# A re-tuned instruction order, with the second W1 split by column halves and exp's bias of two batches on GpSimd

## The chip, the cores and the metric

The kernel runs on one core of a Trainium2 chip. The metric is the device time of one execution, in microseconds (us). A core has five engines with a queue of instructions each: TensorE (PE in the profile, its weight loads PEld), VectorE (DVE), ScalarE (ACT), GpSimd (POOL) and SyncE (SP), which issues all transfers here.

## The reference

Three blocks follow each other, on 4 batches of 576 rows and 512 columns.

```python
# 1. attention, 8 heads of 64, with only the 32 largest scores of a row kept
scores = q @ k.T / 8
kth    = the 32nd largest score of the row
attn   = softmax(where(scores >= kth, scores, -1e9))
x      = attn @ v                                   # heads side by side: (4, 576, 512)
# 2. Fourier mixing and an FFN
u  = x + real(fft(fft(x, axis=1), axis=2))
x  = u + relu(layernorm(u) @ w_ch1) @ w_ch2         # 512 -> 2048 -> 512
# 3. a second FFN with its own weights and a gain g_ln
x  = x + relu(layernorm(x) * g_ln @ w_ch1') @ w_ch2'
```

The weights arrive as 64-bit floats. Products of fp16 pairs (a high and a low half of each value) stand in for fp32 products.

## The kernel before, in words

The function `tile_attention_fourier_ffn` doesn't issue instructions at once. It records them in a `Program`, and a planner (`Program.order`, line 336 on) then places all of them in one fixed order for each engine. At every step it takes, of the instructions whose inputs and buffers are planned to be ready, the one that can start first; among those that could start together the one with the lowest priority number. The planned duration of each instruction comes from `price` (line 289 on), with a doubled price for TensorE when it has had too few columns lately (line 397). Priorities come from the table `LEVELS`: for each named phase five numbers, one for each engine in the order TensorE, VectorE, ScalarE, GpSimd, SP, and five slopes by which the number changes over the phase's instructions. `PACE` gives the earliest times of the loads and splits of weights (first time, step, first time of the split, step), and of the statistics of the inputs (s1 to s3).

The phases are: `p0` to `p3` prepare a head's q, k and v; `a0`, `b0` and so on are the two halves of a batch's attention; `e`, `f`, `c` are the Fourier rows and columns; `g`, `o` the layer norms; `m` the first FFN, `n` the second FFN; `w1a`, `w2a`, `w2b`, `w1b` load and convert the four weights (1a and 2a of the first FFN, 1b and 2b of the second), and `x1a` and so on split them into fp16 halves. In program order each batch's attention comes first, then its Fourier part and norms (`front`), then the two FFNs; the planner mixes the attention of batch b + 1 into the FFNs of batch b.

Attention (`attend`) handles 36 tiles of 128 query rows for a batch. TensorE makes the scores, ScalarE copies them to s, and VectorE finds the 32 largest by four MAX8 (mx) with three replacements between (a value load and a replacement, which write w). Then VectorE makes nb, the bias of exp, from the largest and the 32nd value: one column of 128 rows, shown as `tiny<-mx` (batch 0, whose scale is a constant) or `tiny<-mx,sc` (the others). ScalarE goes on with Prelu (`s<-s,mx`), exp (`s<-s,tiny`), which needs nb, and an fp16 copy p; GpSimd subtracts to get p's low half; SP transposes p to pt, and TensorE multiplies by v (`xp<-vt,pt`).

An FFN works on 256 rows (tiles A and B of a batch) or 128 (C, for the odd rows of two batches). For each of 16 blocks f of 128 hidden columns TensorE adds up 12 matmuls of W1 into a buffer of the tag mm (three buffers), ScalarE and GpSimd (VectorE in the last batch) make the halves of h (two buffers), and TensorE multiplies h by block f of W2. A block f reads W1's columns `fs` of half `f // 8`, for all four blocks `dc` of 128 rows. W1A, W2A and W1B stay in SBUF. W2 of the second FFN is kept in DRAM (W2D) and loaded block by block into tiles of the tag ws.

W1B's memory serves as staging space for the other weights until the fourth weight itself is loaded. That weight is then split in 8 chunks c of 1024 columns: chunk c holds rows block `c // 2` and column half `c % 2`. Each chunk has two parts of 512 columns. For a part ScalarE makes a scaled copy in a tile of the tag ws (`ws<-W1B,tiny`) and its fp16 high half (`W1B<-ws`), and GpSimd subtracts to get the low half (`W1B<-ws,W1B`). The tag ws has two buffers and, unlike the other tags, a single queue for all streams, so that its tiles are handed out in program order: first the raw words of the fourth weight, then the split's 16 parts, then the W2 blocks of the second FFN.

```python
        P.tag(name, nbytes, bufs, split=name != "ws")                       # line 474
        vt.queue = vt.tag.queues.setdefault(self.stream if vt.tag.split else "", [])   # line 284
            t = P.tile("ws", [128, 2, 512], F16)                            # line 1128, W2 of the second FFN
            sp.dma_start(out=t, in_=W2D[f])
```

Of the kernel before, what the change touches and what calls it, by code (L numbers as in the profile page):

```python
# [17 lines left out]
ALU = mybir.AluOpType  # L18
# [50 lines left out]
LEVELS = {'a0': (99, 178, 7, -140, 441, -52, 95, 45, -105, 270), 'a1': (-20, -99, 572, -2, -218, -142, 122, 184, -28, 77), 'a2': (-140, 579, -502, -147, 161, 21, 207, 85, 77, -182), 'a3': (-142, -62, 142, 637, 122, 18, 53, 50, 48, -50), 'const': (231, 276, -510, -32, 217, 199, -207, -198, 71, -11), 'e0': (137, -39, 42, -496, -277, 78, -57, 145, 59, -79), 'e1': (-51, 334, -544, -257, -279, 132, -197, 53, 220, 260), 'e2': (-501, 419, -430, -171, 209, -156, 116, -65, -91, -198), 'e3': (-524, 499, -134, -294, 380, -27, 66, 153, 40, -249), 'f0': (-110, 178, -342, 181, 82, -229, -83, -408, 166, 132), 'f1': (-399, 429, -93, -94, 191, 0, 245, 49, -108, 292), 'f2': (273, -472, -408, 45, 230, 89, 100, 70, 74, 36), 'f3': (-2, 28, 455, -446, -130, -137, 253, -14, 146, 26), 'm0': (75, -18, 248, -377, 396, 74, -225, -112, -24, -36), 'm1': (152, 359, -246, 528, -356, 200, -79, 158, 237, 13), 'm2': (352, -165, -189, -571, -113, -58, -32, -342, 15, -203), 'm3': (-432, -110, 548, -8, 58, 20, -195, -2, 200, -97), 'n0': (309, -620, -101, -184, 37, 84, 20, 312, -12, -64), 'n1': (472, -201, -160, 434, 18, 148, 194, -185, -49, -73), 'n2': (687, -146, -140, 636, 597, 136, 246, -63, -112, -156), 'n3': (670, 195, -133, 501, -300, 192, -83, 35, -158, -54), 'p0': (496, -621, 26, -170, -181, 7, 22, 17, -189, -75), 'p1': (420, 240, 189, 49, 382, -103, -5, -4, 83, -42), 'p2': (-142, 595, 495, 433, 824, -135, 21, 44, -4, -67), 'p3': (-166, 268, 411, -177, 301, -41, -35, 2, -90, -8), 'st0': (-133, -139, -87, -43, -414, -199, -98, -174, -106, 123), 'st1': (226, -333, 107, 35, -411, 99, -86, 312, -76, -15), 'st2': (-218, -203, 88, -366, 295, 123, -208, 4, 20, -60), 'st3': (-10, -68, 146, 208, 57, -189, -296, 99, -5, 22), 'sv0': (445, -86, -414, 331, -306, -171, 81, -18, -39, 91), 'w1a': (-96, -235, 543, 89, 145, -109, 22, 66, -21, 118), 'w1b': (-152, -500, 48, -6, -4, 207, 98, -16, 95, -180), 'w2a': (-334, -79, 25, 129, -16, 11, 130, 47, 14, -322), 'w2b': (-310, 7, 32, -650, -5, -3, 92, -167, -21, 51), 'b0': (-186, 280, -343, 51, 33, -85, 55, -52, 51, 89), 'c0': (-170, -344, -7, -124, -47, 34, 25, 94, -286, -3), 'g0': (364, -83, 534, -267, 171, 160, -53, 31, 173, 97), 'o0': (383, -151, -46, -64, -263, 3, -235, 43, 13, -54), 'b1': (-394, 461, 138, 131, -208, 27, 123, 86, -103, -70), 'c1': (-238, -803, -221, 201, -273, 139, 98, -130, 117, -69), 'g1': (-305, 194, 401, 9, -254, -52, -157, -163, -141, -36), 'o1': (161, 224, 48, -340, 317, -147, 78, 159, -50, -154), 'b2': (177, 545, 171, -131, 9, -139, 122, 156, 137, -47), 'c2': (366, -97, -56, 425, 398, 67, 69, -96, -23, 217), 'g2': (-280, -259, 470, -171, 212, -46, -46, 108, 109, 40), 'o2': (596, 339, -84, 199, 45, 216, 91, -25, -381, -27), 'b3': (-90, 64, -217, 248, 308, 181, 127, 237, 261, 31), 'c3': (689, 64, 316, 592, -294, 57, -175, -53, 117, 1), 'g3': (341, 155, 274, 9, -9, -202, 128, -162, -10, 50), 'o3': (-280, -313, 364, -250, -37, 4, -74, -140, 253, 11), 'x1a': (32, 105, 264, 122, -133, 14, -77, -180, 36, -173), 'x2a': (-423, -381, -359, -381, -276, 19, -71, 333, -45, 227), 'x1b': (-433, -288, 222, 112, 290, -24, -91, -71, -65, 3), 'x2b': (263, -69, 295, 26, -182, 126, -245, 41, 166, -94)}  # L69
PACE = {'1a': (7.0, 4.0, 60.0, 6.5), '2a': (8.0, 5.0, 88.0, 1.5), '2b': (31.0, 10.0, 0.0, 8.5), '1b': (87.0, 14.0, 119.0, 9.5), 's1': (83.0, 4.5, 230, 0.5), 's2': (127.0, 3.0, 670, 8.0), 's3': (3.0, 1.0, 100, 2.5)}  # L70


def rows_ap(t, first, step, n, width):
# [123 lines left out]
class Program:  # L197
# [138 lines left out]
    def order(self):  # L336
# [108 lines left out]
def tile_attention_fourier_ffn(ctx: ExitStack, tc: tile.TileContext, q, k, v, w1a, w2a, g, w1b, w2b, c1_in, c2_in, c2l_in, out):  # L445
# [182 lines left out]
    def load_weight(nm, W, src, raws, tmps, t0, step, t1, step1):  # L628
# [609 lines left out]
```

## Time and profile before

| | |
|---|---|
| time, median of 3 runs | 1324.04 us (1323.81 to 1325.63) |
| the profiled execution's own time | 1330.46 us |
| its span, first to last instruction | 1328.7 us |
| TensorE busy | 1182.6 us, 89% |
| VectorE busy | 993.0 us, 75% |
| ScalarE busy | 846.0 us, 64% |
| GpSimd busy | 680.2 us, 51% |
| mean granted TensorE clock | 0.94 of full speed |

The shares are averages over the whole span, and the stages have different limits, so the rows further down are taken by stretches of time. Busy time is the time in which at least one instruction of the engine is on record; durations of neighbouring records on an engine can overlap. A wait is put down to the instruction that released it. All instructions carry the line of the planner's emit loop, L433, so that tiles' names, not lines, tell the groups apart. Matmul records at the lower of the two clock levels are about twice as long.

### The profile page before, as it was taken

The page shows a single profiled execution, that of the slowest core. Times are in us where ns is not written, and L with a number is a line of the kernel's source. Part 1 is how long each engine was busy: PE and PEld are TensorE (multiplying, and loading weights), DVE is VectorE, ACT ScalarE, POOL GpSimd, SP SyncE. Part 2 cuts the span into 40 slices and gives each one's busy share as a digit, 9 for nine tenths or more (in the row PEclk, how much of TensorE's full clock was granted, in tenths as well). Part 3 has the DMA queues.
Part 4 walks back from the last instruction along what each step waited for, and adds up shares of the span by engine and source line. Part 5 has one row for each costly group of instructions (what it writes and reads, how often), then busy time and mean ns, then how long its engine had stood idle before and what let it go on. Part 6 is the DMA issues. An engine that isn't in the chain of part 4 may idle for free.

```text
span 1328.7 us, 27154 instructions
## 1 busy us (share of the span) xinstructions
PE 1182.6 (89%) x9422; PEld 748.8 (56%) x9422; DVE 993.0 (75%) x2361; ACT 846.0 (64%) x1888; POOL 680.2 (51%) x1015
## 2 busy tenths in 40 slices
PE   7757888676799749999999999979999999999998
PEld 3433444342566525656666766656666666667665
DVE  6999999939899998999967986999996651214112
ACT  4658888467878897787767786777777652122111
POOL 3666343646777776666756564766645452011000
PEclk9999788578799869999999999999999999999999
DMA  6898655978867656876826376699514735014112
GB/s 186 193 263 222 178 129 122 264 189 234 196 162 158 121 120 153 174 170 141 177 62 110 68 175 164 141 217 189 105 22 97 163 90 129 13 24 126 27 33 56
DMA packets 356085, 184.86 MB, mean 139 GB/s; under 512 B 293225, under 2 KB 321002, under 8 KB 355818
## 3 DMA queue, kind: packets, MB, share of 16 engines
q1 hardware_dynamic: 355946, 183.11, 59.0%
q8 instruction: 74, 1.21, 0.4%
q14 instruction: 65, 0.53, 0.1%
HBM read 101.78 MB, written 14.16 MB: 87 GB/s over the span
## 4 chain that ended last, share of the span: by engine, by line
PE 63%; DVE 11%; DMA 7%; ACT 6%; issue 2%; POOL 2%; SPq 2%; POOLq 0%; ACTq 0%; DVEq 0%
PE mm L433 31%; PE acc L433 24%; PE ps L433 4%; PE xp L433 4%; DVE mx L433 4%; DVE w L433 3%; DMA pt<-p 2%; DMA ws<-W2D 2%; ACT s L433 2%; SPq L433 2%; DMA W1B<-in_moe_w_ch_dram 2%; DVE tiny L433 1%; DVE W1B L433 1%; DVE W2A L433 1%; ACT W1B L433 1%
## 5 line engine op out<-in xcount | busy, mean ns | idle before, releaser
L433 DVE MAX8 mx<-w 128x8 f32<-128x576 f32 x432 | 314.3, 747 | 1.3
L433 POOL TENSOR_TENSOR p<-s,p 128x64 f16<-128x64 f32 (+1 forms) x288 | 208.1, 743 | 118.2 <-ACT p L433 106.5
L433 ACT ACTIVATE h<-mm 128x256 f16<-128x256 f32 (+1 forms) x320 | 115.7, 362 | 212.7 <-PE mm L433 181.0
L433 PEld LDWEIGHTS <-h 128*128 128x128 f16 x1728 | 161.7, 98 | 141.6 <-issue 7.0
L433 PE MATMUL mm<-unT,W1B 128*128 128x256 f16 (+1 forms) x1920 | 220.7, 263 | 6.0 <-ACT W1B L433 3.4
L433 PE MATMUL mm<-unT,W1A 128*128 128x256 f16 (+1 forms) x1920 | 221.3, 263 | 1.1 <-DMA unT<-t2k 0.6
L433 PE MATMUL acc<-W2A,h 128*128 128x512 f16 x864 | 216.9, 379 | 1.4 <-POOL h L433 1.2
L433 POOL TENSOR_TENSOR h<-hr,h 128x256 f16<-128x256 f32 (+1 forms) x224 | 143.9, 646 | 140.1 <-ACT h L433 78.9
L433 PEld LDWEIGHTS <-W1B 128*128 128x128 f16 (+1 forms) x1984 | 176.8, 99 | 67.3 <-POOL W1B L433 13.9
L433 DVE MATCH_REPLACE8 w<-mx,w 128x576 f32<-128x576 f32 x288 | 212.8, 740 | 0.0
L433 PEld LDWEIGHTS <-W1A 128*128 128x128 f16 (+1 forms) x1984 | 177.5, 99 | 60.1 <-POOL W1A L433 8.1
L433 PE MATMUL acc<-ws,h 128*128 128x512 f16 x654 | 165.9, 380 | 6.2 <-DMA ws<-W2D 5.6
L433 DVE SCALAR_TENSOR_TENSOR h<-mm,h 128x256 f16<-128x256 f32 (+1 forms) x96 | 36.4, 379 | 171.8 <-ACT h L433 142.9
L433 DVE MAX8 mx<-s 128x8 f32<-128x576 f32 x144 | 107.5, 747 | 53.9 <-ACT s L433 53.6
L433 ACT ACTIVATE s<-s,mx 128x576 f32<-128x576 f32 x144 | 111.0, 773 | 22.2 <-DVE mx L433 21.9
L433 ACT ACTIVATE hr<-mm 128x256 f32<-128x256 f32 (+1 forms) x224 | 82.1, 368 | 65.0 <-PE mm L433 53.8
L433 PE MATMUL xp<-vt,pt 128*128 128x65 f16 (+1 forms) x2240 | 106.0, 203 | 16.5 <-DMA pt<-p 13.7
L433 PEld LDWEIGHTS <-pt 128*128 128x128 f16 (+1 forms) x2240 | 94.6, 107 | 44.9 <-DMA pt<-p 22.9
L433 ACT ACTIVATE s<-ps 128x576 f32<-128x576 f32 x144 | 93.6, 650 | 39.9 <-POOL p L433 21.8
L433 DVE MATCH_REPLACE8 w<-mx,s 128x576 f32<-128x576 f32 x144 | 106.6, 740 | 0.0
L433 PE MATMUL ps<-kt,qt 128*128 128x512 f16 (+5 forms) x512 | 90.2, 320 | 18.3 <-ACT s L433 18.2
L433 ACT ACTIVATE p<-s 128x576 f16<-128x576 f32 x144 | 97.6, 683 | 2.4 <-DMA pt<-p 1.9
(155 smaller groups left out, 1643.2 us busy)
## 6 DMA issues: line engine op xcount, KB each, us to landing
ws<-W2D SPq DMA_DIRECT2D x118, 256.0 KB
W1B<-in_moe_w_ch_dram SPq DMA_DIRECT2D x56, 512.0 KB
n<-in_q_dram SPq DMA_DIRECT2D x32, 128.0 KB
n<-in_k_dram SPq DMA_DIRECT2D x32, 128.0 KB
n<-in_v_dram SPq DMA_DIRECT2D x32, 128.0 KB
W2F<-W1B SPq DMA_DIRECT2D x16, 256.0 KB
ws<-in_moe_w_ch_dram SPq DMA_DIRECT2D x16, 256.0 KB
W1B<-W2F SPq DMA_DIRECT2D x16, 256.0 KB
```

Of the source, the lines that this page charges most:

```text
L433: getattr(getattr(self.nc, op.eng), op.method)(*[fix(a) for a in op.args], **{k: fix(v) for k, v in op.kw.items()})
```

## The change

Four things change.

- The split of the fourth weight (W1B) takes its chunks in the order 0, 2, 4, 6, 1, 3, 5, 7: first the first column half of all four blocks of rows, then the second half. The order in which its tiles of ws are asked for follows.
- nb of batches 0 and 1 is made on GpSimd; batches 2 and 3 keep VectorE.
- Two prices of the planner change: a replacement's fixed part on VectorE from 168 to 112 ns, and TensorE's price after few columns from twice the price to twice the price plus 25 ns.
- All numbers of LEVELS and PACE are replaced, and the Fourier constants may be loaded from 168 us on instead of 183.

In the diff, LEVELS is one long line for each side; of it a few entries are shown, each on a line of its own.

```diff
-SMALL = "dve"
+SMALL = (0, 1)
...
-LEVELS = {
+LEVELS = {
...
-'f1': (-399, 429, -93, -94, 191, 0, 245, 49, -108, 292)
+'f1': (-86, 422, 309, 152, 178, 42, 293, 57, -21, 295)
...
-'p1': (420, 240, 189, 49, 382, -103, -5, -4, 83, -42)
+'p1': (412, -138, 185, 52, 416, -162, 102, -7, 76, -16)
...
-'b1': (-394, 461, 138, 131, -208, 27, 123, 86, -103, -70)
+'b1': (-451, 482, 130, 72, 48, 46, 249, 94, -93, -72)
...
-'x1b': (-433, -288, 222, 112, 290, -24, -91, -71, -65, 3)
+'x1b': (-628, -341, 195, -119, 200, -108, -221, -70, -101, -89)
...
-PACE = {'1a': (7.0, 4.0, 60.0, 6.5), '2a': (8.0, 5.0, 88.0, 1.5), '2b': (31.0, 10.0, 0.0, 8.5), '1b': (87.0, 14.0, 119.0, 9.5), 's1': (83.0, 4.5, 230, 0.5), 's2': (127.0, 3.0, 670, 8.0), 's3': (3.0, 1.0, 100, 2.5)}
+PACE = {'1a': (0.0, 4.5, 8.0, 2.0), '2a': (7.0, 3.5, 120.0, 0.0), '2b': (82.0, 1.5, 0.0, 13.0), '1b': (87.0, 16.0, 0.0, 59.0), 's1': (82.0, 0.5, 230, 0.5), 's2': (16.0, 12.0, 670, 8.0), 's3': (162.0, 10.5, 100, 2.5)}
...
-            op.cost = (168 if op.method == "match_replace" else 76 if op.method in ("tensor_scalar", "tensor_tensor") else 66) + 57 * fields + n / (1.92 if fast else 0.96)
+            op.cost = (112 if op.method == "match_replace" else 76 if op.method in ("tensor_scalar", "tensor_tensor") else 66) + 57 * fields + n / (1.92 if fast else 0.96)
...
                 if columns.get(k - 1, 0) < enough:
-                    op.cost *= 2
+                    op.cost = 2 * op.cost + 25
...
-    sm, rv = getattr(P, SMALL), getattr(P, FLIP)
+    rv = getattr(P, FLIP)
...
-        for c in range(8):
-            P.at(t1 + c * step1, (nm, 2, c))
+        for i, c in enumerate(range(8) if nm != "1b" else (0, 2, 4, 6, 1, 3, 5, 7)):
+            P.at(t1 + i * step1, (nm, 2, i))
...
-            parts = [tmps(2 * c + j) for j in range(2)]
+            parts = [tmps(2 * i + j) for j in range(2)]
...
         nb = tiny(1)
-        sm.tensor_scalar(out=nb, in0=mx[:, 31:32], scalar1=mx[:, 0:1], scalar2=scale(b, "c"), op0=ALU.subtract, op1=ALU.mult)
+        (gp if b in SMALL else dve).tensor_scalar(out=nb, in0=mx[:, 31:32], scalar1=mx[:, 0:1], scalar2=scale(b, "c"), op0=ALU.subtract, op1=ALU.mult)
...
-        P.at(183)
+        P.at(168)
```

## Rows read from the trace of the kernel before

**Rows 1.** Busy time in stretches: PE, PEld, DVE, ACT, POOL, then clock, DMA.

```profile
26.00:133.00 107.00, 75.95 (x402) 38.89 (x400) 104.11 (x235) 74.58 (x138) 67.17 (x67) 1.00 0.85 222
133.00:266.00 133.00, 106.43 (x636) 54.81 (x636) 122.40 (x282) 98.68 (x190) 60.05 (x75) 0.74 0.64 173
...
345.00:451.00 106.00, 104.27 (x943) 71.22 (x943) 101.75 (x256) 87.92 (x205) 76.43 (x118) 0.99 0.70 160
451.00:471.50 20.50, 11.44 (x102) 6.75 (x99) 20.47 (x48) 20.34 (x41) 19.48 (x30) 0.67 0.74 131
471.50:500.00 28.50, 10.91 (x98) 5.65 (x99) 27.86 (x61) 26.08 (x55) 20.46 (x28) 0.64 0.55 113
500.00:1064.00 564.00, 542.88 (x4907) 361.58 (x4907) 476.86 (x1123) 413.80 (x970) 347.37 (x564) 0.99 0.64 137
1064.00:1328.70 264.70, 259.46 (x1970) 174.93 (x1968) 70.49 (x187) 58.89 (x160) 36.13 (x45) 0.99 0.25 63
```

**Rows 2.** Tile ws: durations in ns (min/median/max), first and last start in us.

```profile
L433 PE MATMUL acc<-ws,h x654: 376/379/634, 508.7 to 1305.3; 128*128 128x512 f16 x164
L433 SPq DMA_DIRECT2D ws<-W2D x118: 317/367/1393, 503.3 to 1267.3; - x118
...
L433 ACT ACTIVATE ws<-W1B,tiny x16: 706/713/737, 444.6 to 500.9; 128x512 f32<-128x512 f32 x16
...
L433 POOL TENSOR_TENSOR W1B<-ws,W1B x16: 1155/1161/1290, 452.0 to 503.7; 128x512 f16<-128x512 f32 x16
```

**Rows 3.** Timeline of POOL and PE; busy time with W1B, 451 to 498.4.

```profile
470.38 1.16 POOL L433 TENSOR_TENSOR W1B<-ws,W1B 128x512 f16<-128x512 f32 x1
...
497.19 1.16 POOL L433 TENSOR_TENSOR W1B<-ws,W1B 128x512 f16<-128x512 f32 x1 [1.64 <-ACT ws L433]
...
498.41 0.39 PE L433 MATMUL mm<-unT,W1B 128*128 128x256 f16 x2 [0.71 <-POOL W1B L433]
...
451.00:498.40 47.40, 5.48 (x22) 2.02 (x21) 0.00 (x0) 16.49 (x26) 15.19 (x14) 0.64 0.64 122
```

**Rows 4.** Exp's bias on DVE: tile tiny; timeline (start us, us).

```profile
L433 DVE TENSOR_SCALAR tiny<-mx,sc x108: 235/261/274, 315.9 to 1051.9; 128x1 f32<-128x1 f32 x108
...
L433 DVE TENSOR_SCALAR tiny<-mx x36: 173/200/214, 26.7 to 272.4; 128x1 f32<-128x1 f32 x36
...
67.46 0.20 DVE L433 TENSOR_SCALAR tiny<-mx 128x1 f32<-128x1 f32 x1
67.59 0.75 DVE L433 MAX8 mx<-w 128x8 f32<-128x576 f32 x1
...
447.02 0.24 DVE L433 TENSOR_SCALAR tiny<-mx,sc 128x1 f32<-128x1 f32 x1
...
447.18 1.41 DVE L433 MAX8 mx<-w 128x8 f32<-128x576 f32 x2
```

**Rows 5.** Small instructions on POOL: tiles n and tiny, and one of the timeline.

```profile
L433 POOL TENSOR_SCALAR n<-n,sc x80: 526/535/1375, 14.3 to 959.4; 128x320 f32<-128x320 f32 x80
...
L433 POOL TENSOR_TENSOR tiny<-tiny,mhalf x20: 548/700/875, 309.2 to 1221.0; 128x2 f32<-128x2 f32 x16, 128x1 f32<-128x1 f32 x4
...
48.15 0.12 POOL L433 MEMSET vt<- 128x5 f16 x1
```

**Rows 6.** Tile W1B: one group of DVE's; busy time with W1B, 26 to 500.

```profile
L433 DVE SCALAR_TENSOR_TENSOR W1B<-W1B x24: 666/680/1527, 127.3 to 361.2; 128x512 int32<-128x512 int32 x24
...
26.00:500.00 474.00, 37.90 (x136) 13.23 (x120) 69.81 (x136) 86.27 (x145) 100.48 (x83) 0.85 0.73 182
```

**Rows 7.** Waits: who waited for whom, us in total, times, longest.

```profile
ACT s L433 <- DVE tiny L433: 10.9, 9, 4.3
```

**Rows 8.** Timeline of DVE and PE: a replacement with its load; 28 matmuls.

```profile
61.30 0.08 DVE L433 MATCH_VALUE_LOAD w<-mx,w 128x8 f32 x1
...
62.03 0.08 DVE L433 MATCH_VALUE_LOAD w<-mx,s 128x8 f32 x1
...
462.99 1.69 PE L433 MATMUL xp<-vt,pt 128*128 128x65 f16 x28 [2.57 <-ACT xB L433]
```

More of the change, by code (lines that the diff above doesn't have):

```diff
@@ L67 @@
 CONV = {"1a": ("dve", "dve"), "2a": ("dve", "dve"), "1b": ("dve", "dve"), "2b": ("dve", "dve")}
-LEVELS = {'a0': (99, 178, 7, -140, 441, -52, 95, 45, -105, 270), 'a1': (-20, -99, 572, -2, -218, -142, 122, 184, -28, 77), 'a2': (-140, 579, -502, -147, 161, 21, 207, 85, 77, -182), 'a3': (-142, -62, 142, 637, 122, 18, 53, 50, 48, -50), 'const': (231, 276, -510, -32, 217, 199, -207, -198, 71, -11), 'e0': (137, -39, 42, -496, -277, 78, -57, 145, 59, -79), 'e1': (-51, 334, -544, -257, -279, 132, -197, 53, 220, 260), 'e2': (-501, 419, -430, -171, 209, -156, 116, -65, -91, -198), 'e3': (-524, 499, -134, -294, 380, -27, 66, 153, 40, -249), 'f0': (-110, 178, -342, 181, 82, -229, -83, -408, 166, 132), 'f1': (-399, 429, -93, -94, 191, 0, 245, 49, -108, 292), 'f2': (273, -472, -408, 45, 230, 89, 100, 70, 74, 36), 'f3': (-2, 28, 455, -446, -130, -137, 253, -14, 146, 26), 'm0': (75, -18, 248, -377, 396, 74, -225, -112, -24, -36), 'm1': (152, 359, -246, 528, -356, 200, -79, 158, 237, 13), 'm2': (352, -165, -189, -571, -113, -58, -32, -342, 15, -203), 'm3': (-432, -110, 548, -8, 58, 20, -195, -2, 200, -97), 'n0': (309, -620, -101, -184, 37, 84, 20, 312, -12, -64), 'n1': (472, -201, -160, 434, 18, 148, 194, -185, -49, -73), 'n2': (687, -146, -140, 636, 597, 136, 246, -63, -112, -156), 'n3': (670, 195, -133, 501, -300, 192, -83, 35, -158, -54), 'p0': (496, -621, 26, -170, -181, 7, 22, 17, -189, -75), 'p1': (420, 240, 189, 49, 382, -103, -5, -4, 83, -42), 'p2': (-142, 595, 495, 433, 824, -135, 21, 44, -4, -67), 'p3': (-166, 268, 411, -177, 301, -41, -35, 2, -90, -8), 'st0': (-133, -139, -87, -43, -414, -199, -98, -174, -106, 123), 'st1': (226, -333, 107, 35, -411, 99, -86, 312, -76, -15), 'st2': (-218, -203, 88, -366, 295, 123, -208, 4, 20, -60), 'st3': (-10, -68, 146, 208, 57, -189, -296, 99, -5, 22), 'sv0': (445, -86, -414, 331, -306, -171, 81, -18, -39, 91), 'w1a': (-96, -235, 543, 89, 145, -109, 22, 66, -21, 118), 'w1b': (-152, -500, 48, -6, -4, 207, 98, -16, 95, -180), 'w2a': (-334, -79, 25, 129, -16, 11, 130, 47, 14, -322), 'w2b': (-310, 7, 32, -650, -5, -3, 92, -167, -21, 51), 'b0': (-186, 280, -343, 51, 33, -85, 55, -52, 51, 89), 'c0': (-170, -344, -7, -124, -47, 34, 25, 94, -286, -3), 'g0': (364, -83, 534, -267, 171, 160, -53, 31, 173, 97), 'o0': (383, -151, -46, -64, -263, 3, -235, 43, 13, -54), 'b1': (-394, 461, 138, 131, -208, 27, 123, 86, -103, -70), 'c1': (-238, -803, -221, 201, -273, 139, 98, -130, 117, -69), 'g1': (-305, 194, 401, 9, -254, -52, -157, -163, -141, -36), 'o1': (161, 224, 48, -340, 317, -147, 78, 159, -50, -154), 'b2': (177, 545, 171, -131, 9, -139, 122, 156, 137, -47), 'c2': (366, -97, -56, 425, 398, 67, 69, -96, -23, 217), 'g2': (-280, -259, 470, -171, 212, -46, -46, 108, 109, 40), 'o2': (596, 339, -84, 199, 45, 216, 91, -25, -381, -27), 'b3': (-90, 64, -217, 248, 308, 181, 127, 237, 261, 31), 'c3': (689, 64, 316, 592, -294, 57, -175, -53, 117, 1), 'g3': (341, 155, 274, 9, -9, -202, 128, -162, -10, 50), 'o3': (-280, -313, 364, -250, -37, 4, -74, -140, 253, 11), 'x1a': (32, 105, 264, 122, -133, 14, -77, -180, 36, -173), 'x2a': (-423, -381, -359, -381, -276, 19, -71, 333, -45, 227), 'x1b': (-433, -288, 222, 112, 290, -24, -91, -71, -65, 3), 'x2b': (263, -69, 295, 26, -182, 126, -245, 41, 166, -94)}
@@ L70 @@
-PACE = {'1a': (7.0, 4.0, 60.0, 6.5), '2a': (8.0, 5.0, 88.0, 1.5), '2b': (31.0, 10.0, 0.0, 8.5), '1b': (87.0, 14.0, 119.0, 9.5), 's1': (83.0, 4.5, 230, 0.5), 's2': (127.0, 3.0, 670, 8.0), 's3': (3.0, 1.0, 100, 2.5)}
+LEVELS = {'a0': (29, 91, -11, -61, 548, -33, 228, 55, -88, 360), 'a1': (-68, -84, 530, -114, 70, -84, 139, 210, -163, -23), 'a2': (-71, 634, -592, -137, 236, -61, 228, 188, 98, -66), 'a3': (-373, -70, 180, 652, 82, 5, 88, 130, -42, -51), 'const': (-646, -411, 322, -122, -234, -225, -17, -188, -6, -72), 'e0': (177, -452, 48, -317, 346, 79, -27, 70, 89, 159), 'e1': (68, 232, -453, -340, -361, 106, -171, 61, -125, 248), 'e2': (-210, 431, -273, -163, 149, 36, -76, -86, -205, -145), 'e3': (-642, 459, -360, -396, 406, -6, -33, -205, -98, -254), 'f0': (227, 214, -490, 229, -330, 126, -12, -350, 99, 171), 'f1': (-86, 422, 309, 152, 178, 42, 293, 57, -21, 295), 'f2': (-449, -721, -711, -308, -352, -1, -105, 37, 39, -208), 'f3': (121, -85, 347, -348, 82, -207, 296, -116, 45, 39), 'm0': (416, -94, 408, -355, -132, 23, -243, -154, 282, -277), 'm1': (120, 322, -308, 297, -192, 130, 121, 317, 206, -67), 'm2': (143, -351, -298, -694, -126, 205, -54, 61, 93, -149), 'm3': (-329, -237, 487, -24, 432, -100, -35, -80, 158, -103), 'n0': (220, -654, -214, -203, -27, 72, -247, 300, -262, 291), 'n1': (380, -273, -249, 276, -111, 37, -209, 109, 67, -260), 'n2': (743, 43, -146, 600, 588, 202, 72, -60, -201, -78), 'n3': (589, 36, -281, 426, -574, 109, -34, -145, 69, 2), 'p0': (464, 328, 27, -221, -75, 150, 120, 13, -93, -65), 'p1': (412, -138, 185, 52, 416, -162, 102, -7, 76, -16), 'p2': (510, 528, 430, 450, 741, -157, -86, 65, -41, -48), 'p3': (-309, 227, 325, -308, 286, -115, 103, -26, -164, -104), 'st0': (-296, 248, -259, -363, -458, -258, -121, -176, -107, 193), 'st1': (113, 145, 78, 218, -348, 50, -92, 96, 191, -26), 'st2': (-178, -246, 104, 54, 324, 147, -57, 284, 53, 54), 'st3': (-35, -92, -17, 48, 43, -197, -256, 33, -30, 21), 'sv0': (-370, -220, -575, 102, -513, -146, 57, 88, 33, 46), 'w1a': (-4, -156, 665, 138, 243, -211, 64, -135, 258, -44), 'w1b': (399, -434, 193, 16, 233, 326, 6, -56, 110, 54), 'w2a': (-233, -95, 132, 135, 73, -8, 72, -70, 61, 73), 'w2b': (-444, -87, 58, -247, -111, -19, 34, -222, 5, 113), 'b0': (-207, 322, -350, -34, -129, -162, 6, -21, 163, 235), 'c0': (-265, -304, 162, 6, -51, 41, 72, 122, -221, 1), 'g0': (233, -145, 198, -559, 43, 158, -112, 2, 93, 88), 'o0': (351, -181, -81, 12, 200, -51, -281, -5, 37, -192), 'b1': (-451, 482, 130, 72, 48, 46, 249, 94, -93, -72), 'c1': (-196, 274, -277, 204, -27, 186, 22, -187, -52, -37), 'g1': (491, 98, 403, 152, -10, -155, -88, -112, 59, -118), 'o1': (-389, 397, 467, 237, 451, -206, 17, -332, 68, 48), 'b2': (-108, 661, 461, -404, -46, 16, 264, 125, 119, -4), 'c2': (-71, -303, -472, 230, 97, -31, 85, -100, -119, 167), 'g2': (-57, -367, -217, -137, -181, 154, 42, 72, 295, -68), 'o2': (431, -484, 1, 191, -282, -133, -335, 57, -379, 42), 'b3': (6, -206, -182, 197, 337, 358, 187, 149, 150, 61), 'c3': (67, -766, 345, 622, -161, -55, -128, 242, -218, 9), 'g3': (339, -208, 241, -12, -215, -68, -81, 63, 15, -113), 'o3': (263, 265, -553, -658, -171, 5, 102, -35, -80, -15), 'x1a': (-111, 148, 520, 99, -108, -13, -86, 6, 65, -1), 'x2a': (-480, -68, -228, -342, -296, 63, -26, 351, 33, -264), 'x1b': (-628, -341, 195, -119, 200, -108, -221, -70, -101, -89), 'x2b': (309, -169, 184, -403, -120, 61, 120, 97, 10, -126)}
```

## The prediction

> **What bounds the kernel now.** I read the page's slices first, then the busy time of each engine in stretches [rows 1], because shares over the whole span mix stages with different limits. The reader should see four stages there. From 26 to 266 us VectorE is the limit: 104.1 of 107 and 122.4 of 133 us, 226.5 of 240 in all, while TensorE waits for work. From 345 to 451 us the first FFN pass of batch 0 keeps TensorE busy for 104.3 of 106 us, and VectorE, with the top-32 search of batch 1, for 101.8. Then there is a hole. From 451 to 500 us TensorE works only 22.4 of 49 us, at a granted clock of about 0.65, a mix of its two levels of 1.2 and 2.4 GHz, while VectorE is busy for 48.3 and ScalarE for 46.4 of these 49 us. After 500 us TensorE is the limit to the end: 542.9 of 564 and 259.5 of 264.7 us. So whatever fills the hole, or lets the TensorE-bound part begin sooner, should come off the end nearly whole; a gain on VectorE after 500 us is worth little by itself.
>
> The next view is the tile view of the split, which says who makes the hole. The second FFN of batch 0 needs the split W1B. The 16 parts of that split run from 444.6 to 504.9 us: ScalarE's first scaled copy starts at 444.6, and GpSimd's last subtraction starts at 503.7 and takes 1.16 [rows 2]. In the order of time [rows 3] GpSimd's 7th part starts at 470.38 and its 13th at 497.19. TensorE's wait before its W1B matmuls ends at 498.41, released by GpSimd's W1B, just when the 13th part is done (497.19 + 1.16 = 498.35). That fits the code: f = 0 reads the first columns of all four blocks of rows, chunks 0, 2, 4 and 6, and chunk 6 begins with the 13th part.
>
> But a second gate follows. The tag ws has two buffers and one queue for all streams, in the order of the program (line 474), and the second FFN's blocks of W2 come through the same tag (line 1128). The first of these loads is issued at 503.3, when the 15th part has given its buffer back, and the first matmul on it starts at 508.7 [rows 2].
>
> **The change, part by part.**
>
> *Halves of columns.* In the new order chunk 6 comes fourth, so f = 0 to 3 would be free after the 7th part, at 470.38 + 1.16 = 471.5 in the old pace, 27 us sooner. Yet the second half of each f waits for ws, and the order of ws is untouched: all 16 parts still come first. With three mm and two h buffers TensorE can do three blocks of 12 matmuls ahead and no more. Of these 36 matmuls 22 were done before 498.4 us already, in 5.5 us [rows 3]. What moves into the idle stretch is the other 14, at 5.48 / 22 = 0.25 us 3.5 us at the most at that clock, half of it at the full one. I take 2 us. The bounds are 0 and the whole idle time from 471.5 to 500, 28.5 - 10.9 = 17.6 us, plus what the low clock costs there, 10.9 x (1 - 0.64) = 3.9 us: 21.5 us.
>
> *exp's bias on GpSimd.* It takes 36 instructions of batch 0 and 36 of batch 1 off VectorE. Their records last 0.20 us for batch 0 (x36) and 0.26 us for the others (x108), but records overlap; from their start to the next one's start it is 67.59 - 67.46 = 0.13 and, rounded, 447.18 - 447.02 = 0.17 us [rows 4]. So VectorE is relieved of 36 x 0.13 = 4.7 us in batch 0 and 36 x 0.17 = 6.1 us in batch 1. Batch 0's part lies in the stage that VectorE bounds: I take all 4.7 (bounds 0 and 36 x 0.20 = 7.2). Batch 1's lies largely where TensorE is full or the split is late: I take half, 3 us (bounds 0 and 36 x 0.26 = 9.4).
>
> GpSimd's price for this form is not in the trace. A memset of 5 columns takes 0.12 us, the 320-column tensor_scalar 0.535 us by its median, the tiny pow 0.70 [rows 5]. The bounds are 0.12 and 0.70; nearest is the tensor_scalar with far fewer columns, so I take 0.31, an estimate between the memset and that row. 72 x 0.31 = 22 us fit into the idle time of GpSimd, which was busy for 243.6 of the 395 us of the five stretches listed between 26 and 500 us [rows 1]. The cost is nothing while that cover lasts. But exp now waits for a second hop, behind whatever is ahead in GpSimd's queue, subtractions of 1.16 us among them [rows 3], and ScalarE's copy of p, its evacuations of h and the split's copies are queued behind exp; GpSimd's p and SP's transpose wait for them. Prelu goes ahead of exp and covers the usual delay. ScalarE waited for this bias for only 10.9 us in nine places so far [rows 7]. I charge 2 us (bounds 0 and 36 x 0.70 = 25).
>
> GpSimd and VectorE also share a way into SBUF. In the trace, VectorE's two-input W1B conversion takes 0.68 us by the median but up to 1.53 [rows 6], so something does hold it at times. The Trainium skill, "Perfetto Trace Analysis", section "Optimizing Scalar/DVE Operations", says that the two share an SBUF read port, "so offloading operations between those two might not help". By that rule the 22 us of bias meet VectorE's weight conversions, 69.8 of 474 us [rows 6], so 22 x 0.147 = 3.3 us would be lost and the sum below would be 8.4 instead of 11.7; the long maximum agrees with it without showing who held it.
>
> *Priorities and paces.* These reorder every queue, and the trace can't show the new orders. What I can cost is the place of the hole. On ScalarE front(1) (f1) went from -93 to 309, while the split (x1b) stays near 200: it now goes ahead of the front; on GpSimd it goes from 112 to -119, ahead of b1, f1 and p1. In the old trace the first seven parts start (470.38 - 452.0) / 6 = 3.06 us apart, the last nine (503.7 - 470.38) / 9 = 3.70 [rows 2, 3]. At the first pace throughout, the last part comes 9 x 0.64 = 5.8 us sooner, and so does the first W2 load. I take 4 us, since ScalarE is nearly full there; bounds -6, if the front is then late, and 17.6, all of the idle time. The chunk pace of 59 us lets the last chunk begin at 7 x 59 = 413 us, before 444.6, so it delays nothing. What is late next is the W2 load itself, 5.4 us from issue to matmul.
>
> For the rest of the order I take 0, and as bounds the idle time after 500 us, 564 - 542.9 = 21.1 us, halved or doubled. Two prices of the planner change too. VectorE's value load and replacement take 62.03 - 61.30 = 0.73 us [rows 8]; the old price is 0.768, the new one 0.712, so VectorE is planned better. A low-clock PV matmul takes 1.69 / 28 = 0.06 us [rows 8], and the added 25 ns makes that too dear. Neither decides.
>
> **The sum.** 2 + 4.7 + 3 - 2 + 4 = 11.7 us. The profiled execution took 1330.46 us, its span 1328.7; so it becomes 1318.8. It stands 6.4 us over the median of 1324.04, and from the median the same sum gives 1312.
>
> **The rivals.**
> - *The hole closes.* If the new order brings the W1B loads and the whole split some 25 us forward, ws is free too: 21.5 + 4.7 + 3 = 29 us, so 1295. For it: nothing but W1B and ws holds TensorE there. Against it: ScalarE and VectorE are at 95% or more in the hole, so the split's work must push something out.
> - *Nothing to see.* The ws gate stays at 503, the relief of VectorE is spent in waits that end elsewhere, and the front loses what the split gains: 1324. For it: the ws queue is unchanged.
> - *The bias holds ScalarE.* This ends on the other side. The place is ScalarE from 345 to 500 us, busy for 134.3 of 155 us, so 20.7 us of slack. If exp waits w longer in each of batch 1's 36 tiles, the delay is 36 w - 20.7, against 10.7 us of gains that stand; it decides from w = 0.9 us. One subtraction ahead in the queue (1.16) makes w = 1.2: 43.2 - 20.7 - 10.7 = 12 us slower, 1336. For it: GpSimd is busy for 95% of 451 to 471.5 us. Against it: Prelu covers most of such a wait.
> - *The order after 500 us is worse.* Idle time there doubles: 21.1 - 11.7 = 9.4 us slower, 1333. For it: all priorities of batches 1 to 3 moved. Against it: TensorE has work in reserve for most of that stretch.
>
> **How the numbers follow.** My forecast has 0.48, with a range of its own of 1301 to 1321 from its terms' bounds taken in part. The closed hole has 0.15, no change 0.13, the held ScalarE 0.13, the worse order 0.11. About 0.2% (2.6 us) is what a measurement here can tell from no change. So faster has 0.48 + 0.15 = 0.63, the same 0.13, slower 0.13 + 0.11 = 0.24. The range from 1291 to 1334 takes in the closed hole and the worse order and leaves out most of the held ScalarE and the far ends.
>
> **What would show it.** Right: 72 bias records on GpSimd of 0.2 to 0.4 us; f = 0 of the second FFN released by the 7th part; the first W2 load still right behind the 15th part, but 4 to 8 us sooner; TensorE over 22.4 us busy in the 49 us before it. Wrong: ScalarE's waits for the bias well over 11 us in batches 0 and 1; the W2 load as late as 503 or later; idle TensorE time after 500 us far from 21 us, which would mean that the reordering, and not these parts, sets the result.

## The result and the profile after

The change makes the kernel slower: 1334.58 us (median of 4 runs, 1332.43 to 1335.93) against 1323.92 us for the kernel before (median of 4), a ratio of 1.0081 [1.0058, 1.0105]. A second series gave 1334.99 against 1324.83 us and 1.0060 [1.0034, 1.0085]. The forecast was 1312 us and faster; the time lies just above the top of its range of 1291 to 1334. Executions of one kernel spread by about 1%: 32 of the kernel before took 1319.41 to 1332.55 us. Here and below the ratios, with their 95% intervals, are not the quotients of the two medians; the two can differ by up to 0.24%.

The profiled execution took 1332.43 us, its span 1330.6. The same stretches as in [rows 1] (start and end, length, then PE, PEld, DVE, ACT, POOL, clock, DMA):

```profile
26.00:133.00 107.00, 81.04 (x403) 42.66 (x402) 106.16 (x231) 76.57 (x143) 69.65 (x86) 0.60 0.81 213
133.00:266.00 133.00, 101.93 (x667) 53.73 (x666) 119.19 (x265) 100.08 (x191) 67.32 (x97) 0.77 0.72 183
345.00:451.00 106.00, 97.47 (x881) 64.09 (x878) 100.72 (x242) 87.82 (x200) 84.57 (x139) 0.98 0.69 147
451.00:471.50 20.50, 9.80 (x81) 5.49 (x81) 20.39 (x49) 19.75 (x43) 16.33 (x25) 0.58 0.61 126
471.50:500.00 28.50, 17.95 (x147) 10.95 (x145) 24.22 (x51) 27.91 (x56) 24.96 (x33) 0.68 0.45 97
500.00:1064.00 564.00, 539.64 (x4818) 354.62 (x4819) 467.12 (x1104) 407.22 (x958) 344.24 (x563) 0.99 0.64 134
1064.00:1330.60 266.60, 260.42 (x1983) 177.33 (x1981) 64.43 (x173) 54.96 (x149) 34.84 (x43) 1.00 0.27 65
```

The hole from 451 to 500 us is a little less empty: TensorE works 9.80 + 17.95 = 27.8 us of 49, against 22.4. But the stretch ahead of it, which was full, has lost 104.27 - 97.47 = 6.8 us. From 500 to 1064 us TensorE is busy for 3.2 us less, and the end comes later. The granted clock of the first stretch, 0.60 here and 1.00 in [rows 1], goes with the execution and not with the order: over the same stretch it is 0.61 and 0.98 in two traces of the old order told below, whose spans are both 1320.1 us, and 0.93 in a second trace of the changed kernel.

The tile ws (ns as min/median/max, first and last start):

```profile
L433 PE MATMUL acc<-ws,h x654: 376/379/634, 500.0 to 1307.5; 128*128 128x512 f16 x164
L433 SPq DMA_DIRECT2D ws<-W2D x118: 319/332/1321, 497.4 to 1269.5; - x118
L433 ACT ACTIVATE ws<-W1B,tiny x16: 705/715/729, 449.8 to 495.4; 128x512 f32<-128x512 f32 x16
L433 POOL TENSOR_TENSOR W1B<-ws,W1B x16: 1151/1157/1167, 453.8 to 497.7; 128x512 f16<-128x512 f32 x16
```

Exp's bias, the tile tiny, which now stands on GpSimd for batches 0 and 1:

```profile
L433 POOL TENSOR_SCALAR tiny<-mx x36: 283/294/732, 27.6 to 263.8; 128x1 f32<-128x1 f32 x36
L433 POOL TENSOR_SCALAR tiny<-mx,sc x36: 357/367/832, 306.2 to 535.2; 128x1 f32<-128x1 f32 x36
```

The timeline of GpSimd and of TensorE in that stretch:

```profile
453.81 2.28 POOL L433 TENSOR_TENSOR W1B<-ws,W1B 128x512 f16<-128x512 f32 x2
...
470.25 2.27 POOL L433 TENSOR_TENSOR W1B<-ws,W1B 128x512 f16<-128x512 f32 x2
...
479.79 2.27 POOL L433 TENSOR_TENSOR W1B<-ws,W1B 128x512 f16<-128x512 f32 x2
...
481.00 0.40 PE L433 MATMUL mm<-unT,W1B 128*128 128x256 f16 x1 [0.61 <-POOL W1B L433]
...
496.18 1.16 POOL L433 TENSOR_TENSOR W1B<-ws,W1B 128x512 f16<-128x512 f32 x1 [1.38 <-ACT ws L433]
...
499.98 1.89 PE L433 MATMUL acc<-ws,h 128*128 128x512 f16 x4 [2.37 <-ACT p L433]
```

Two parts of the split come at 453.8, then none for 14 us, then the rest. The 7th part is the first of the pair at 479.79; it ends at 479.79 + 1.16 = 480.95, and TensorE's wait ends at 481.00: the halves do free f = 0 with the 7th part, 17 us sooner than in [rows 3] (498.41). Yet the first W2 load is issued at 497.4 and its first matmul starts at 500.0 ([rows 2]: 503.3 and 508.7). The same line in two more traces of the old order (one with the split by halves only, one with a second bias that nobody reads, both told below) and in a second trace of the changed kernel:

```profile
L434 SPq DMA_DIRECT2D ws<-W2D x118: 318/362/1924, 500.6 to 1258.7; - x118
L435 SPq DMA_DIRECT2D ws<-W2D x118: 318/354/1394, 497.3 to 1258.7; - x118
L433 SPq DMA_DIRECT2D ws<-W2D x118: 319/332/1390, 499.3 to 1273.5; - x118
```

The first FFN begins sooner. Its W1 matmuls in the kernel before, then in the changed one (first and last start):

```profile
L433 PE MATMUL mm<-unT,W1A x1920: 217/272/421, 345.5 to 1217.5; 128*128 128x256 f16 x154, 128*128 128x128 f16 x38
L433 PE MATMUL mm<-unT,W1A x1920: 216/272/421, 319.4 to 1218.2; 128*128 128x256 f16 x154, 128*128 128x128 f16 x38
```

Where the time goes needs one more measure, since busy time hides a low clock and slow slots. For every kernel I take TensorE's columns at 2.4 GHz (in full stretches 128x512 matmuls follow each other 0.216 us apart; 512 / 2.4 = 0.213) and subtract them from the time: the rest is time lost. The columns come to 1095 us in all kernels; how the columns of fp32 matmuls are counted moves the first number of each row of the table alike, and no difference between rows. Of one profiled execution each, the time lost in us:

| kernel | to 345 us | 345 to 525 | 525 to the last matmul | sum |
|---|---|---|---|---|
| before (the profile of the rows) | 121.3 | 49.9 | 57.3 | 228.5 |
| old order, halves only | 119.5 | 46.8 | 53.6 | 219.9 |
| old order, bias doubled | 116.7 | 47.1 | 56.1 | 219.9 |
| changed | 108.6 | 56.0 | 66.1 | 230.7 |
| changed, second series | 109.7 | 59.5 | 65.5 | 234.7 |

The second and third rows are experiments that take as long as the kernel before; they show its order in executions of 1320.1 us span, where the profile of the rows, with 1328.7, was a long one. Against the mean of these two the new order is 9 us ahead at 345 us, loses 11 us to 525 us, and 11 us more behind that. One execution doesn't hold such a number to better than some 3 us: in seven traces of the old order the time lost behind 525 us runs from 53.6 to 60.2 us, with a mean of 57.5, and against that mean the new order loses 8 us there.

### The profile page after: what moved, and what is told of

It is laid out like the page before. It is cut to its first block, busy times and chain, and to the rows that moved or that the text cites. A ratio compares the mean times of both kernels' runs of the same rounds, so it can differ in the third digit from the quotient of the medians.

```text
span 1330.6 us, 27195 instructions
## 1 busy us (share of the span) xinstructions
PE 1184.4 (89%) x9422; PEld 748.1 (56%) x9422; DVE 978.1 (74%) x2289; ACT 845.9 (64%) x1888; POOL 704.3 (53%) x1087
## 4 chain that ended last, share of the span: by engine, by line
PE 53%; DVE 22%; DMA 11%; ACT 7%; POOL 3%; issue 3%; SPq 1%; POOLq 0%; DVEq 0%; ACTq 0%
PE mm L433 26%; PE acc L433 20%; DVE mx L433 8%; DVE w L433 7%; DMA pt<-p 5%; PE ps L433 4%; PE xp L433 3%; ACT s L433 2%; DMA ws<-W2D 2%; DVE W1B L433 2%; DVE tiny L433 2%; POOL p L433 1%; DMA W1B<-in_moe_w_ch_dram 1%; DVE W1A L433 1%; ACT p L433 1%
## 5 line engine op out<-in xcount | busy, mean ns | idle before, releaser
L433 PE MATMUL mm<-unT,W1B 128*128 128x256 f16 (+1 forms) x1920 | 226.5, 265 | 6.3 <-ACT h L433 2.2
L433 PE MATMUL acc<-ws,h 128*128 128x512 f16 x654 | 169.3, 383 | 10.6 <-DMA ws<-W2D 7.2
L433 PE MATMUL ps<-kt,qt 128*128 128x64 f16 (+5 forms) x512 | 89.5, 320 | 19.1 <-ACT s L433 16.7
L433 ACT ACTIVATE p<-s 128x576 f16<-128x576 f32 x144 | 97.5, 684 | 10.9 <-DMA pt<-p 10.3
```

Of the source, the lines that this page charges most:

```text
L433: getattr(getattr(self.nc, op.eng), op.method)(*[fix(a) for a in op.args], **{k: fix(v) for k, v in op.kw.items()})
```

## The experiments

"The old order" is the order of the kernel before, kept instruction by instruction: only the engine or the operands of the instructions named change where they are issued. "The new order" is that of the changed kernel, kept in the same way. So each run differs from its base in what is named and in nothing that the planner would move. The diffs say what an edit does in effect; the code itself sets the engine or the operands where an instruction is issued. Of the theories in the expectations, 1 says that the new order alone makes the loss, and 2 that the move of the bias does, by exp's wait for GpSimd; the letters are explained where they stand.

**The parts alone, and the bias taken back.**

```diff
 # old order, bias: nb of batches 0 and 1
-                getattr(self.nc.vector, "tensor_scalar")(out=nb, ...)
+                getattr(self.nc.gpsimd, "tensor_scalar")(out=nb, ...)
 # old order, halves: the split's parts read and write the chunk of the new order
-  in_=wf[:, c * 1024 + j * 512:...], scale=gs[:, c // 2:c // 2 + 1]
+  in_=wf[:, d * 1024 + j * 512:...], scale=gs[:, d // 2:d // 2 + 1]   # d = (0, 2, 4, 6, 1, 3, 5, 7)[c]
 # new order, bias back
-                getattr(self.nc.gpsimd, "tensor_scalar")(out=nb, ...)
+                getattr(self.nc.vector, "tensor_scalar")(out=nb, ...)
```

Old order, bias on GpSimd: 

> The old order of all queues, every buffer as before; only exp's bias of batches 0 and 1 is issued on GpSimd, at the place in the order that it had on VectorE. Theory 1 (the new order alone makes the change slower): within 0.3% of before, 1320 to 1328 us, ScalarE's waits for the bias below 20 us. Theory 2 (the bias holds ScalarE): 8 us or more slower, 1332 us or above, with ScalarE's waits for the bias of batches 0 and 1 at 25 us or more. My forecast's own term: 5 to 6 us faster, 1318.

Measured: 1334.23 against 1322.02 us, ratio 1.0101 [1.0077, 1.0125]. The time is that of theory 2. The waits are not: exp waits 14.7 us for its bias, below the 25 that theory 2 asked for and the 20 that theory 1 allowed.

Old order, halves only: 

> The old order; only which column half each of the split's 16 parts handles is changed (chunks 0, 2, 4, 6 first). Theory 1: no measurable change, 1321 to 1327 us, because the first W2 load still waits for the 15th part; the matmuls of blocks 0 to 2 of the second FFN may end earlier. If the order of the chunks itself were the gain that the hole suggests: 1300 to 1310 us.

Measured: 1322.57, ratio 1.0009 [0.9992, 1.0027].

Old order, both: 

> The old order with both edits: everything of the change but its priorities, paces and prices. Theory 1: 1317 to 1328 us, so that what is left to the changed kernel's 1334.6 is the order alone, 7 to 17 us. Theory 2: as slow as the changed kernel, 1332 us or more.

Measured: 1333.97, ratio 1.0103 [1.0079, 1.0126].

New order, bias back on VectorE: 

> The changed kernel's order, every buffer as there; only exp's bias of batches 0 and 1 is issued on VectorE again, at the place in the order that it has on GpSimd. Theory 1: as slow as the changed kernel or a little slower, 1333 to 1342 us. Theory 2: 8 us or more faster than the changed kernel, 1327 us or less.

Measured: 1343.52, ratio 1.0172 [1.0140, 1.0205].

So in the old order the halves are worth nothing, alone or with the bias (no run takes them out of the new one), and the bias is worth opposite things: moving it costs the old order 12 us, and moving it back costs the new one 9 us by the medians (1343.5 against 1334.6) and 12 to 15 by the ratios, since the two stood in different series. Each order is best with the engine it was planned for. The waits of ScalarE for the bias from 26 to 560 us agree; first the old order with the bias on VectorE and a second one on GpSimd (the run told next), then with the bias on GpSimd, then the changed kernel, then the new order with the bias back on VectorE:

```profile
ACT s L435 <- DVE tiny L435: 6.3, 3, 4.3
```

```profile
ACT s L434 <- POOL tiny L434: 14.7, 15, 5.2
```

```profile
ACT s L433 <- POOL tiny L433: 4.0, 6, 1.5
```

```profile
ACT s L434 <- DVE tiny L434: 10.5, 13, 2.7
```

**Batch 0, batch 1, and GpSimd's time by itself.**

```diff
-        if b in (0, 1): on GpSimd
+        if b == 0: on GpSimd            # one run
+        if b == 1: on GpSimd            # another
 # third run: the bias stays on VectorE, and GpSimd makes a second one that nobody reads
+        self.nc.gpsimd.tensor_scalar(out=nb2, ...)   # for batches 0 and 1
```

> The old order, exp's bias of batch 0 alone on GpSimd. If the cost of the move (12 us for both batches, measured) comes from the stage before 275 us: 8 to 12 us slower than before, 1330 to 1334. If it comes from ScalarE between 345 and 500 us, as my rival had it: within 3 us of before. My forecast's term for this batch alone: 4.7 us faster.

Measured: 1328.18 against 1324.83, ratio 1.0025 [1.0006, 1.0044].

> The old order, exp's bias of batch 1 alone on GpSimd. If the cost comes from the stage before 275 us: within 3 us of before. If it comes from ScalarE between 345 and 500 us: 8 to 12 us slower, 1330 to 1334. My forecast's term for this batch alone: 3 us faster.

Measured: 1331.99, ratio 1.0056 [1.0031, 1.0082].

> The old order; exp's bias stays on VectorE and is read from there, and right behind each of the 72 of batches 0 and 1 GpSimd makes the same column once more, for nobody to read. Theory A (GpSimd's queue is held, because it now stops at each bias until VectorE's search is done, and what stands behind it in the queue is late): most of the 12 us come back, 1329 to 1336, with GpSimd waiting some 16 us for VectorE's mx as in the kernel with the moved bias. Theory B (exp waits for GpSimd): within 3 us of before, 1319 to 1325.

Measured: 1324.62, ratio 0.9996 [0.9977, 1.0014].

The changed kernel once more, beside them: 

> The changed kernel once more, for a second trace of the same order: 1332 to 1337 us. If its blocks of the FFN come at the same times as in the first trace within 3 us, the first trace stands for the kernel; the old order's two traces differ by 8.6 us from 620 us on.

Measured: 1334.99, ratio 1.0060 [1.0034, 1.0085].

Neither batch alone makes the cost: 3.4 us with batch 0 and 7.2 with batch 1, each outside both of the ranges that its expectation gave. Exp's waits for GpSimd in these two runs, batch 0 first:

```profile
ACT s L434 <- POOL tiny L434: 9.0, 8, 5.2
ACT s L434 <- POOL tiny L434: 5.1, 7, 1.6
```

The larger waits go with the smaller cost, so the sum of the waits doesn't price the move. The 72 instructions on GpSimd cost nothing as long as nobody waits for them. What costs is that exp waits for them: 14.7 us in fifteen waits, 9.5 of them before 300 us, the longest 5.2, and GpSimd in its turn waits for VectorE's mx. GpSimd's waits from 26 to 500 us, in the old order with the bias on GpSimd and then with the second bias that nobody reads:

```profile
POOL tiny L434 <- DVE mx L434: 16.1, 8, 6.4
POOL nb L437 <- DVE mx L435: 16.8, 9, 6.5
```

GpSimd is held as long in both, and only the first run is slower; so theory A, the held queue, falls, and theory B, exp's wait, stands. Two of exp's waits on ScalarE's timeline in the first run:

```profile
69.55 0.77 ACT L434 ACTIVATE s<-s,tiny 128x576 f32<-128x576 f32 x1 [1.38 <-POOL tiny L434]
...
437.43 0.87 ACT L434 ACTIVATE s<-s,tiny,sc 128x576 f32<-128x576 f32 x1 [1.55 <-POOL tiny L434]
```

The 16.1 and 16.8 us are GpSimd's: in the old order the bias comes at the place in the plan that VectorE's had, so GpSimd, which takes its instructions in order, stands before it until mx is there.

**Where the new order loses: switched to the old order at four points.** The instructions that the plan starts before the point come in the new order, all others in the old one; the split by halves and the bias on GpSimd stay. By the new prices the planner plans the same end for these orders within 1.0 us: 1280.5 us for the new order, and 1280.5, 1280.8, 1281.5 and 1280.8 for the four. The kernel before has a planned end of 1280.9 us, but by its own prices.

```diff
+RANK = ...   # place of each of the 14,955 instructions: new order if planned before T, else old order
-                for op in avail[e]:
+                for op in seq[e][-1:]:      # only the next one by RANK
```

> The changed kernel with its new order kept for everything that the plan starts before 430 us (4,435 of 14,955 instructions; some 445 us on the chip), and the old order for all the rest; the split by halves and the bias on GpSimd stay as in the change. The plan ends at 1280.5 us, as those of the old and the new order do. Theory L (the new order loses after some 500 us): the second part is the old one, so the time is near the old order's 1322 to 1325 us, and the waits of the running sums on W2's transfers from 600 to 1066 us fall back to some 3 to 4 us. Theory E (the loss is laid in the early part, by what the new order has moved or left behind at 445 us, and only shows later): 1332 to 1336 us, as the changed kernel.

Measured: 1324.58 against 1325.84, ratio 1.0006 [0.9987, 1.0025].

> As the run that switches at 430 us, with the switch at 505 us of the plan (5,292 instructions before it; some 525 us on the chip), so that the end of the split of W1B and the first W2 load are in the new order too. Plan's end 1280.8 us. Theory L: 1321 to 1326 us. Theory E: 1332 to 1336 us. If the stretch from 445 to 525 us is what costs, this run is slower than the one that switches at 430 us by the whole 8 to 12 us.

Measured: 1325.41, ratio 1.0005 [0.9985, 1.0026].

> As before, with the switch at 750 us of the plan (8,893 instructions before it; some 780 us on the chip); plan's end 1281.5 us. Theory L with a loss spread evenly from 500 to 1064 us: half of the 12 us, 1327 to 1330 us. Theory L with one bad stretch: either 1322 to 1325 or 1332 to 1336 us, which says on which side of 780 us it lies. Theory E: 1332 to 1336 us.

Measured: 1330.82, ratio 1.0042 [1.0018, 1.0066].

> As before, with the switch at 900 us of the plan (11,009 instructions before it; some 935 us on the chip); plan's end 1280.8 us. Theory L with an even loss: 1330 to 1333 us. Theory E: 1332 to 1336 us. A time near 1323 us would put the whole loss behind 935 us.

Measured: 1330.36, ratio 1.0058 [1.0035, 1.0081].

Theory L holds, and theory E falls: with the new order up to some 445 or 525 us and the old one behind it, the change costs nothing, and also gains nothing. The loss enters behind 525 us, some 5 us of it by 780 us. How the rest divides is not resolved: the switch at 900 is 0.5 us below the switch at 750 by its median and above it by its ratio, which is already that of the changed kernel's second series (1.0058 and 1.0060). The time lost by TensorE behind 525 us rises in the same order: 56.4 us with the switch at 430, 58.7 at 505, 60.3 at 750, 62.6 at 900, 66.1 in the changed kernel; of these only the last two lie clearly above what the old order's own traces show (up to 60.2).

**Why the lead is lost, and whether W2's transfers make the loss.** In these three the 118 transfers through ws are left out, and the matmuls read a wrong weight that is in SBUF already.

```diff
-            sp.dma_start(out=t, in_=W2D[f])                        # t of the tag ws
...
-                    pe.matmul(out=acc[:, tt, :], lhsT=h[...], rhs=w[:, c, :], ...)
+                    pe.matmul(out=acc[:, tt, :], lhsT=h[...], rhs=W2A[:, f][:, c, :], ...)
```

Old order: 

> The kernel before in its own fixed order, with the 118 transfers ws<-W2D left out; the matmuls of the second FFN that read them read the first FFN's second weight instead, so this weight is the wrong one and only the times are read. In the old order the first matmul mm<-unT,W1B needs the 15th of the 16 parts of the split, so the hole before 500 us stays whether W2 is there or not. Both theories: the 3 to 5 us of waits on these transfers behind 525 us go, 1317 to 1322 us. It is the base for the two runs beside it.

Measured: 1316.60 us against 1324.37 for the kernel before, ratio 0.9942 [0.9922, 0.9962]. (In the old order f = 0 waits for the 13th part and not for the 15th [rows 3], and the first of these matmuls starts earlier still, at 451 us; the argument doesn't rest on it.)

New order: 

> The changed kernel in its own fixed order, with the same transfers left out and the same wrong weight read. Theory W (what the new order loses behind 525 us is its longer waits on W2's transfers): TensorE's time behind 525 us beyond its columns at full clock falls from 66 us to within 3 us of that of the run beside it in the old order, and so the rest of the 9 to 12 us that the new order loses there goes. Theory S (the loss is many small waits and slower slots of all kinds): 6 us or more of it stay. The hole before 500 us may close in part, since mm<-unT,W1B begins at 474 us here; that is read from the stretch 445 to 525 us by itself.

Measured: 1325.27, ratio 1.0008 [0.9988, 1.0028].

Switched at 430 us: 

> The run that switches to the old order at 430 us of the plan, with the same transfers left out and the same wrong weight read. Theory G (the 10 us that the new order is ahead at 345 us are lost because the second FFN can't begin before W2's first transfer, which has to wait for the last part of the split in the same two buffers): with that transfer gone the lead survives, and this run is 6 to 12 us faster than the old order without the transfers. Rival (the lead is lost because there is no other work at 445 to 500 us, gate or no gate): within 3 us of it.

Measured: 1318.07, ratio 0.9966 [0.9942, 0.9990].

Theory W falls: without these transfers the new order is still 8.7 us slower than the old one, and TensorE loses 60.1 us behind 525 us against 50.0, so the difference of about 10 us stays there. Theory G falls too: with W2's gate gone the early lead does not survive either (1318.1 against 1316.6 us). The waits of TensorE from 400 to 525 us in that last run show what holds it. Its profiled execution was a long one, 1329.7 us against a median of 1318.1, so the sizes are rough:

```profile
PE ps L442 <- ACT s L442: 11.9, 6, 3.9
PE mm L442 <- DMA sq<-in_k_dram: 7.8, 4, 3.0
PE mm L442 <- DMA sq<-in_v_dram: 7.7, 4, 3.1
...
PE mm L442 <- ACT W1B L442: 1.8, 1, 1.8
PE mm L442 <- POOL W1B L442: 0.8, 1, 0.8
```

In its fixed order TensorE stands in the hole before work of the next batches, for their inputs (sq) and for ScalarE's copies of scores (s); W1B itself holds it for 2.6 us. The old order without the transfers waits for the same things, 6.2 and 5.0 us for sq and 7.4 for s; that the lead goes into the longer waits fits, and is not shown by a run.

TensorE's waits from 525 to 1064 us, first in the changed kernel and then in the old order with the halves only:

```profile
PE acc L433 <- DMA ws<-W2D: 6.4, 6, 2.0
PE xp L433 <- DMA pt<-p: 4.8, 7, 1.0
PE ps L433 <- ACT s L433: 2.9, 5, 1.2
PE mm L433 <- ACT h L433: 2.2, 5, 0.9
PE acc L433 <- POOL h L433: 2.0, 5, 0.8
```

```profile
PE xp L434 <- DMA pt<-p: 6.7, 8, 1.9
PE acc L434 <- DMA ws<-W2D: 4.0, 8, 1.2
PE ps L434 <- ACT s L434: 2.0, 2, 1.4
PE mm L434 <- ACT h L434: 1.9, 3, 0.7
PE acc L434 <- POOL h L434: 1.5, 2, 1.2
```

No wait stands out. By the kind of matmul, the time up to the next matmul's start beyond its own columns grows, from old to new order in two pairs of traces, by 4.1 and 5.5 us for mm<-unT,W1B, 3.8 and 2.7 for ps and 1.1 and 2.9 for mm<-unT,W1A, and falls by 2.9 and 1.3 for xp. For acc<-ws,h it grows by 3.1 in one pair and falls by 2.5 in the other. Nor does the growth keep its place: without W2's transfers it is 6.3 us for acc<-W2A,h and 3.7 for mm<-unT,W1A, and below 1 us for mm<-unT,W1B and ps.

## Why the prediction was wrong, point by point

- **Halves of columns, -2 us.** Measured 0 in the old order (1.0009 [0.9992, 1.0027]). The mechanism was right, the gate too: f = 0 is released by the 7th part, and the first W2 load is still issued just as the last part but one gives its buffer back (496.18 + 1.16 = 497.34, when that subtraction ends, and 497.4). Nothing of the 2 us reaches the end. One reading was off: TensorE goes four blocks ahead of W2, not three; 48 matmuls on W1B start before the first on W2 in the changed kernel, and 47 are on record there in the kernel before.
- **The bias of batches 0 and 1 on GpSimd, -4.7 - 3 + 2 = -5.7 us.** The price was near: 0.29 and 0.37 us against my estimate of 0.31. The wait was mis-sized: that Prelu "covers the usual delay" does not hold in the old order, where exp's waits for its bias rise from 6.3 to 14.7 us and the kernel takes 12 us longer. (The 10.9 us that I read count all four batches; up to 560 us it was 6.3 in three waits.) There the rival "The bias holds ScalarE" has the sign and, with 1336 us, the size; but not by 1.2 us in each tile of batch 1: there are fifteen waits, 9.0 us of them with batch 0 alone, which costs 3.4 us, and 5.1 us with batch 1 alone, which costs 7.2. In the new order the waits are 4.0 and 2.5 us, less than with VectorE in the old one, and taking the bias off GpSimd costs 9 us or more. I wrote a sum of a relief and a wait; the runs show that the sign depends on the order. That it is a question of whether GpSimd is free at that moment is my reading, which no run shows by itself.
- **The shared way into SBUF.** By the rule that I cited, the Trainium skill, "Perfetto Trace Analysis", section "Optimizing Scalar/DVE Operations", I estimated that 3.3 us would be lost. The run with the doubled bias puts the same 72 instructions beside VectorE's work and measures 0.9996 [0.9977, 1.0014]; 3.3 us would be 1.0025. VectorE's busy time with W1B from 26 to 500 us is 70.87 us there, between the 69.81 of [rows 6] and 71.22 with the halves only. No cost of this kind shows here.
- **The split earlier, -4 us.** The pace came as worked out: the last subtraction starts at 497.7 instead of 503.7, 6.0 us sooner where 5.8 stood, at (497.7 - 453.8) / 15 = 2.93 us a part, although the split pauses for 14 us. But the base was wrong. The two other traces of the old order have the first W2 load at 500.6 and 497.3 us, the changed kernel has it at 497.4 and 499.3. So the 503.3 belonged to one long execution, and nothing was gained that is clear of this spread. I had noted that this execution stood 6.4 us over the median and still priced a place in it to 4 us.
- **What is late next.** I expected W2's load to be the next gate and the idle time before it to shrink by what comes sooner. The first FFN does begin sooner: its first matmul starts at 319.4 us, against 345.5 in the profile of the rows and 342.9 and 339.7 in the two other traces of the old order. But W1B isn't ready sooner, and the lead is spent before 525 us: 345 to 451 us loses 6.8 us of TensorE's busy time. The run with the early new order and the old one behind it shows it: 1324.58 against 1325.84 us, and in its trace 56.3 us lost from 345 to 525 us, where the old order's traces lose 47 to 53. That ScalarE and VectorE were both "at 95% or more in the hole" was read too high for ScalarE: 46.4 of 49 us, and 26.08 of 28.5 in its second part.
- **"For the rest of the order I take 0."** This is the step that failed and that decides. With the same early order, the same halves and the same bias on GpSimd, the kernel takes 1324.6 and 1325.4 us with the old order behind some 445 and 525 us, and 1334.6 and 1335.0 with the new one: the new order behind 525 us costs some 10 us by the medians, 7 to 10 by the ratios and 8 to 11 by TensorE's lost time. The rival "The order after 500 us is worse" gave 1333 us; 1334.6 was measured. Its place was right. Its mechanism, doubled idle time, was not: idle time from 500 to 1064 us goes from 21.1 to 564 - 539.6 = 24.4 us, and the rest is in slower slots of the matmuls and small waits of several kinds. Which decision of the order makes them stays open: W2's transfers are ruled out as the main one; the price changes, PACE and LEVELS were not tried apart; and the new late part was not tried behind the old early one.
- **The signs.** Bias records of 0.29 and 0.37 us on GpSimd, f = 0 released by the 7th part, the first W2 load right behind the 15th and 5.9 us sooner, and 27.8 us of TensorE in the 49 before it: all the signs that I named for being right came, and none of those for being wrong (the changed kernel waits 4.0 us for its bias, loads W2 at 497.4, and is idle for 24.4 us from 500 to 1064 us). The time went the other way all the same. Four signs looked into the hole, and the only one behind it was idle time, which rose by 3.3 us where the time lost rose by 8 to 11.

So of the forecast of -11.7 us: the halves gave 0, the bias and the early order together a lead of 9 us at 345 us that the hole takes back, and the late order, put at 0, costs some 10.

## What to carry to other kernels

A planned end does not price an order to 10 us: five orders whose planned ends agree within 1.0 us take 1324.6 to 1335 us on the chip. Nor may planned ends be compared across price tables: 1280.9 us before and 1280.5 after stand for different prices, and when the kernel's own planner, given the new prices, is made to keep the old order, it ends at 1293.8 us. By its own measure the new order is 13 us better, and the chip takes 11 us more. An instruction moved to an idle engine is judged by who waits for it: put a copy there that nobody reads (which tells the engine's time), then let the consumer read it (which tells the wait). Before a place in a profile is priced to a few microseconds, look at the same place in a second execution of the same order.

## What was not expected of the hardware

A tensor_scalar on one column of 128 rows takes 0.29 us on GpSimd with one scalar read from a tile (batch 0) and 0.37 us with two (batch 1), against 0.20 and 0.26 us on VectorE [rows 4]: by its record GpSimd is 40 to 50% dearer on this form, where its small pow takes 0.70 [rows 5]. From one start to the next the gap is wider: 0.36 us in the two lines below, from the changed kernel, against 0.17 on VectorE [rows 4], whose records overlap more. And seventy-two of them, unread, changed the time of the kernel by a ratio of 0.9996 [0.9977, 1.0014].

```profile
456.07 0.37 POOL L433 TENSOR_SCALAR tiny<-mx,sc 128x1 f32<-128x1 f32 x1
456.43 1.04 POOL L433 TENSOR_SCALAR n<-n,sc 128x320 f32<-128x320 f32 x2
```
